# Sorted-block attention feeding a cosine-gated feed-forward: other products, copies and load order for the sorted keys

## The chip, the cores and the metric

The kernel runs on one NeuronCore of one Trainium2 chip. The metric is the device time of one launch in microseconds (us). The core has a matrix engine (TensorE, PE in the profile; its weight loads are a row of their own, PEld), VectorE (DVE), ScalarE (ACT), GpSimd (POOL) and SyncE (SP, which here only issues DMAs). Matrix products are written to PSUM, and VectorE or ACT copy them to the on-chip memory SBUF; GpSimd works on SBUF alone.

## The reference

```python
def _attn_ref(q, k, v, sort_net):                 # (4, 8, 768, 64) each; sort_net (4, 8, 8, 8)
    P = sort_net
    for _ in range(5):                            # balance rows and columns
        P = np.exp(P - np.max(P, axis=-1, keepdims=True))
        P = P / (np.sum(P, axis=-1, keepdims=True) + 1e-09)
        P = P / (np.sum(P, axis=-2, keepdims=True) + 1e-09)
    # k_b, v_b, q_b: 8 blocks of 96 tokens each
    k_sorted = np.einsum('bhij,bhjcd->bhicd', P, k_b)
    v_sorted = np.einsum('bhij,bhjcd->bhicd', P, v_b)
    scores = scale * np.matmul(q_b, k_sorted.transpose(0, 1, 2, 4, 3))
    attn = softmax(scores)                        # within a block
    return np.matmul(attn, v_sorted).reshape(B, H, S, D)

x = attn_out.transpose(0, 2, 1, 3).reshape(3072, 512)
h = x @ w_in                                      # (512, 2048)
out = (h * np.cos(h)) @ w_out                     # (2048, 512)
```

## The kernel before

**Chunks.** The work is cut into eight chunks n = 0 to 7, two for each of the four batches: half of a batch's eight blocks, all eight heads, 384 tokens. For a chunk, `qk` and `qk_half` make the scores of a block u (two head groups, hp = 0 and 1, of four heads h2), `expo` the softmax's exponentials, `av` the weighted values, `moe_up` or `up` the first matrix of the feed-forward with its cosine gate, `moe_down` or `down` the second and the store. The attention of chunk n + 1 is laid by hand between the feed-forward products of chunk n; the order in the file is the order on each engine, which runs its instructions in that order. Waits between engines follow from the tiles. `B` and `C` are the two PSUM pools, `big` with three buffers and `acc` with two; a tile that finds no buffer free waits for the copy that empties the oldest.

**Keys.** The balanced matrix P is laid out as a block-diagonal matrix `bds`; a product with the keys as weights sorts and transposes at once: it takes two tokens (2 x 64 columns) of all blocks and gives, for one block position and head, 64 dims of the first token on PSUM's partitions 0 to 63 and of the second on 64 to 127. The tile `kT[0]` has three zones along its second axis; for scores, head group hp reads zones hp and hp + 1, dims on partitions hp x 64 upward, so that even tokens come from the first of the two and odd ones from the second. For batch 0, `k_sort_0(ih, ...)` works one chunk ih at a time: one product for each two tokens, of 64 rows (batch 0's keys lie on partitions 64 to 127 of `kbuf`), and four copies of 64 partitions for each PSUM tile, two of them from one partition half to the other. It is called four times for chunk 0 (16, 8, 16 and 8 token pairs), at the head of the attention, and three times for chunk 1 (16 pairs each), between the `up` calls of chunk 0. Scores of chunk 0 read only the 64 rows of their own head group. From chunk 1 on the queries lie between zeros, and a score product reads all 128 rows of two zones; what lies in the other half is multiplied by zero, and `z_keys` clears zones 0 and 2 there so that what is multiplied is finite.

For batch 1, `k_sort_1` makes products of 128 rows, in which the matrix holds zeros against batch 0's, and one copy a tile, into zones 0 and 2 with both tokens one above the other; `k_swap` then moves two quarters into zone 1 by two DMAs on SyncE's queue. The same crossing serves batches 2 and 3 (`k_sort_g`, tile `kT2`, which lies over `kT[0]`).

**Loads.** Loads with a change of type go through GpSimd's DMA queue (`load`, `load_pair`, `load_q`, `load_w_in`, `load_w_out`), so they are issued in GpSimd's order, among its copies: `v_permute` regroups the values, `zeros_between` clears what lies between the queries. The keys and values of batches 2 and 3 come as "the second pair". The second pair's values go to `vbuf` in six pieces, right after `v_permute(slice(64, 128))` has read batch 1's values. Chunk 3's query rows come behind them (`load_q(3)`, eight DMAs), and SyncE turns them by two transposing DMAs (`q_transpose_dma(3)`), ahead of the transposing DMAs for chunk 2's softmax (issued in `expo`, line 518) in its queue.

A small trick is used to hold a queue: a GpSimd copy of one column of a tile into `held` makes GpSimd wait until the tile has been written, and all that stands behind it in GpSimd's order with it.

Of the kernel before, what the change touches and what calls it, by code (L numbers as in the profile page):

```python
# [10 lines left out]
FP32 = mybir.dt.float32  # L11
# [7 lines left out]
def kernel(  # L19
# [15 lines left out]
    nc = tc.nc  # L35
    B, H, S, D = q.shape
# [7 lines left out]
    CD = blk * D  # L44
    H2 = H // 2
    NG = B // 2
    NN = 2 * H2 * nb
    IC = 4
# [23 lines left out]
    vbuf, kbuf = kv[:, :CD], kv[:, CD:]  # L72
# [17 lines left out]
    vin_d = v.rearrange("b h (j c) d -> b (h j) (c d)", j=nb)  # L90
# [4 lines left out]
    def load_pair(buf, src, lo, hi):  # L95

        nc.gpsimd.dma_start(
            out=buf[:, lo:hi], in_=src[2:4].rearrange("b r x -> (b r) x")[:, lo:hi])
# [11 lines left out]
    def q_zeroed(n):  # L110

        return kbuf[:blk, :2 * (QZ + D)] if n % 2 else q_mem[:]
# [3 lines left out]
    def where(n):  # L116
        b, ih = n // 2, n % 2
        return b // 2, b % 2, ih

    def load_q(n):  # L120
        b, ih = n // 2, n % 2
        if n < NQ:

            nc.gpsimd.dma_start(
                out=q_rows, in_=q[b][:, ih * IC * blk:(ih + 1) * IC * blk].rearrange(
                    "h (p r) d -> p h (r d)", r=QR))
        else:
            src = q[b].rearrange("h (i c) d -> c i h d", c=blk).rearrange(
                "c i (h e) d -> c i h e d", e=2)
            q_heads = q_zeroed(n).rearrange("p (e x) -> p e x", e=2)[:, :, :QZ].rearrange(  # L130
                "p e (i h w) -> p i h e w", i=IC, h=H2)[:, :, :, :, :D]
            for i in range(IC):
                for e in range(2):
                    nc.gpsimd.dma_start(  # L134
                        out=q_heads[:, i, :, e], in_=src[:, ih * IC + i, :, e])
# [4 lines left out]
    def zeros_between(n):  # L140
        for x in (D, QZ):
            nc.gpsimd.memset(
                q_zeroed(n)[:, x:x + QZ].rearrange("p (x w) -> p x w", w=2 * D)[:, :, :D], 0.0)
# [16 lines left out]
    def load_w_out(z):  # L160
        c = slice(z * FC // 4, (z + 1) * FC // 4)
        nc.gpsimd.dma_start(out=w_out_t[:, c], in_=w_out_d[:, c])
# [23 lines left out]
    kT, kT2 = [kTs[:, :, 0], kTs[:, :, 2]], kTs[:, :, :2]  # L186
# [4 lines left out]
    for i in range(NP):  # L191
        t = const.tile([blk, 2 * H2, 128], BF16, name=f"p_buf{i}")
# [43 lines left out]
    bds = [const.tile([128, 2 * H, nb], BF16, name=f"bd{g}") for g in range(NG)]  # L236
# [49 lines left out]
    def copy_on(eng, dst, src):  # L286
        if eng is nc.scalar:
            eng.copy(dst, src)  # L288
        else:
            eng.tensor_copy(dst, src)  # L290

    V, A = nc.vector, nc.scalar
# [24 lines left out]
    def q_transpose(n, z, engs, pool, tag):  # L317
        for eng, (dst, src) in zip(engs, q_turn(n, z, pool, tag)):
            copy_on(eng, dst, src)
# [8 lines left out]
    held = const.tile([128, 1], FP32, name="held")  # L328
# [28 lines left out]
    MH = H2 * IC  # L357

    def k_products(ps, t, c, rows, rhs, keys=kbuf):
        nc.tensor.matmul(  # L360
            ps[:, t], keys[rows, c * 2 * D:(c + 1) * 2 * D], rhs, start=True, stop=True)

    def k_sort_0(ih, t0, nt, eng, pool, tag):

        ps = pool.tile([128, nt, 2 * MH], FP32, name="ks", tag=tag)
        for t in range(nt):
            k_products(ps, t, t0 + t, slice(64, 128),
                       bds[0][64:, H:, ih * IC:(ih + 1) * IC])
        ms, ts = slice(ih * MH, (ih + 1) * MH), slice(t0, t0 + nt)
        psv = ps.rearrange("p t (e m) -> p e m t", e=2)  # L370
        for hp in range(2):
            for x in range(2):
                copy_on(eng, kT[0][hp * D:(hp + 1) * D, hp + x, ms, ts],
                        psv[x * D:(x + 1) * D, hp])

    k_open = {}

    def k_first(t0, nt, pool, tag):
        ps = pool.tile([128, nt, 2 * MH], FP32, name="ks", tag=tag)
        for t in range(nt):  # L380
            k_products(ps, t, t0 + t, slice(64, 128), bds[0][64:, H:, :IC])
        k_open[t0] = ps.rearrange("p t (e m) -> p e m t", e=2), slice(t0, t0 + nt)

    def k_place(t0, hp, eng):
        psv, ts = k_open[t0]
        for x in range(2):
            copy_on(eng, kT[0][hp * D:(hp + 1) * D, hp + x, :MH, ts],
                    psv[x * D:(x + 1) * D, hp])

    def k_sort_1(t0, eng, pool, tag):  # L390
        ps = pool.tile([128, 8, 2 * NB], FP32, name="ks", tag=tag)
# [14 lines left out]
    def k_swap(keys):  # L406
        nc.sync.dma_start(out=keys[:64, 1], in_=keys[64:, 0])
        nc.sync.dma_start(out=keys[64:, 1], in_=keys[:64, 2])

    def keys_of(n, u, h2, hp):  # L410
        g, b2, ih = where(n)
        z = slice(hp, hp + 2)
        if n < 2:
            return kT[0][:, z, ih * MH + h2 * IC + u]
        m = h2 * nb + ih * IC + u
        return kT[1][:, z, m] if g == 0 else kT2[:, z, b2, m]

# [15 lines left out]
    def v_turn(eng=A):  # L433
        ps = big.tile([128, 128], FP32, name="bdp", tag="big")
        for r in (0, 64):
            nc.tensor.matmul(
                ps[r:r + 64], ident[:, 64 - r:128 - r], bds[0].rearrange("p x i -> p (x i)"),
                start=True, stop=True)
        copy_on(eng, bdv.rearrange("p x i -> p (x i)"), ps[:])
# [4 lines left out]
    def v_sort_b(b, d0, nd, eng, pool, tag):  # L444
        ps = pool.tile([128, nd, 2 * NB], FP32, name="vs", tag=tag)


        rows, xs = slice(0, 64 + b * 64), slice((1 - b) * H, (2 - b) * H)
        for t in range(nd):
            nc.tensor.matmul(  # L450
                ps[:, t], v_cols(d0 + t, b == 1 or d0 + t >= D // 2)[rows],
                bdv[rows, xs].rearrange("p x i -> p (x i)"), start=True, stop=True)
        copy_on(
            eng, vS[0][:, b * 2 * NB:(b + 1) * 2 * NB, d0:d0 + nd],
            ps[:blk].rearrange("p t n -> p n t"))
# [71 lines left out]
    def p_transpose(n, u, eng, pool, tag):  # L527
        p = pb.pop((n, u))
        ps = pool.tile([128, 2 * H2, 128], BF16, name="pps", tag=tag)
        for a in range(2 * H2):  # L530
            nc.tensor.transpose(ps[:blk, a, :blk], p[:, a, :blk], ident[:blk, :blk])  # L531
        copy_on(eng, pT[n, u][:blk], ps[:blk, :, :blk])
# [44 lines left out]
    def up(n, fp, lo=0, hi=TC):  # L577

        h = big.tile([128, 2, 512], FP32, name="h", tag="big")
        w = hi - lo  # L580
        for f2 in range(2):
            f = fp * 2 + f2
            for kk in range(KC):
                nc.tensor.matmul(  # L584
                    h[:, f2, :w], w_in_t[:, kk, f * 128:(f + 1) * 128], xT[n][:, kk, lo:hi],
                    start=(kk == 0), stop=(kk == KC - 1))
        c = cosp.tile([128, 2, TC], FP32, name="c", tag="c")
        nc.scalar.activation(c[:, :, :w], h[:, :, :w], AF.Sin, bias=half_pi[:, 0:1])  # L588
        if lo == 0:
            gt[n, fp] = gp.tile([128, 2, TC], BF16, name="gg", tag="gg")  # L590
        nc.vector.tensor_tensor(  # L591
            gt[n, fp][:, :, lo:hi], c[:, :, :w], h[:, :, :w], op=ALU.mult)
# [51 lines left out]
    B, C = (big, "big"), (acc, "acc")  # L644
# [10 lines left out]
        balance(1)  # L655
        spread(1)

    def z_keys():
        nc.gpsimd.memset(kT[0][64:, 0], 0.0)
        nc.gpsimd.memset(kT[0][:64, 2], 0.0)  # L660

    def z_vperm():
        nc.gpsimd.memset(vperm[:64, :D // 2 * blk], 0.0)

# [16 lines left out]
    load_w_out(1)  # L681
    load_w_out(2)
    load_w_out(3)
    k_sort_0(0, 0, 16, V, *C)
    v_turn()
    k_sort_0(0, 32, 8, V, *B)
    k_sort_0(0, 16, 16, A, *C)
    k_sort_0(0, 40, 8, A, *C)
    v_sort_b(0, 0, 8, A, *C)
    qk(0, 0)  # L690
    qk(0, 1)
# [22 lines left out]
    z_turned(0)  # L714
    last_balance()
    z_vperm()
    z_keys()
    p_transpose(0, 3, V, *C)
    up(0, 0, 0, 2 * blk)
    p_transpose(0, 2, V, *C)  # L720
    up(0, 1, 0, 2 * blk)
    av(0, 2, True)
    up(0, 2, 0, 2 * blk)
    k_sort_0(1, 0, 16, A, *C)
    av(0, 3, True)
    up(0, 3, 0, 2 * blk)
    x_transpose(0, 2, A, *C)
    up(0, 4, 0, 2 * blk)
    up(0, 5, 0, 2 * blk)
    x_transpose(0, 3, A, *C)  # L730
    k_sort_0(1, 16, 16, V, *C)
    up(0, 6, 0, 2 * blk)
    q_transpose(1, 0, (V, V), *C)
    up(0, 7, 0, 2 * blk)
    k_sort_0(1, 32, 16, A, *C)
    up(0, 0, 2 * blk, TC)
    q_transpose(1, 1, (V, V), *C)
    up(0, 1, 2 * blk, TC)
# [11 lines left out]
    load_pair(pair, kin_d, 0 * CD // 2, 1 * CD // 2)  # L750
    load_pair(pair, kin_d, 1 * CD // 2, 2 * CD // 2)
    v_permute(slice(64, 128))
    load_pair(vbuf, vin_d, 0 * CD // 6, 1 * CD // 6)
    load_pair(vbuf, vin_d, 1 * CD // 6, 2 * CD // 6)
    load_pair(vbuf, vin_d, 2 * CD // 6, 3 * CD // 6)
    load_pair(vbuf, vin_d, 3 * CD // 6, 4 * CD // 6)
    load_pair(vbuf, vin_d, 4 * CD // 6, 5 * CD // 6)
    load_pair(vbuf, vin_d, 5 * CD // 6, 6 * CD // 6)
    expo(1, 0, True)
    expo(1, 1, True)  # L760
    down(0, 0, 0, nc.sync)
# [25 lines left out]
    q_transpose(2, 0, (V, V), *B)  # L787
    q_transpose(2, 1, (V, V), *B)
    zeros_between(3)
    load_q(3)  # L790
    up(1, 0)
    v_sort_b(1, 0, 8, A, *C)
# [111 lines left out]
    ts, w = TC // 128 - 1, Dm // 2  # L904
    for z in range(2):
# [6 lines left out]
        for e, (eng, dma) in enumerate((((A, nc.scalar),), ((V, nc.sync), (A, nc.scalar)))[z]):  # L912
            c = slice(e * w // 2, (e + 1) * w // 2) if z else slice(0, w)
# [32 lines left out]
```

## Time and profile before

| what | value |
|---|---|
| three runs | 249.28, 247.25, 249.14 us; median 249.14 |
| the profiled execution | 247.64 us, of which 245.9 span |
| mean granted TensorE clock | 0.949 of full |
| busy over the span | PE 231.3 us (94%), DVE 175.1 (71%), ACT 159.2 (65%), POOL 88.2 (36%) |
| chunk 0's keys, products and copies | 12.79 to 17.04 us |
| chunk 1's keys | 33.4 to 41.8 us |
| batch 1's crossing, issue to the landing of its second DMA | 62.12 to 72.61 us |

The page cuts the span into 40 slices and gives the busy share of each engine; it also lists the chain of work that ended last, followed back from the end, and groups of instructions by line, with what ended the idle time before them. A copy by the helper `copy_on` shows as line 288 (on ACT) or 290 (on VectorE), so it is told apart by its tiles: `kTs<-ks` are the sorted keys. A key product is line 360 (`ks`), a score product line 422 for chunk 0 and 427 otherwise (`sc`). DMAs that GpSimd issues show as POOL instructions with the line of the `dma_start`: 97 for the second pair's, 134 for query rows.

### The profile page before, as it was taken

Reading aid. Unit: us, or ns where it says so; the run is one execution under the profiler, and the core shown is the slowest. Engines: PE = TensorE matmul, PEld = TensorE weight load, DVE = VectorE, ACT = ScalarE, POOL = GpSimd, SP = SyncE. Lnnn points to the kernel's source line nnn. Section 1 sums busy time; section 2 is a strip of 40 time slices with the busy share of each in tenths; the row PEclk is TensorE's granted clock in tenths of the full one; section 3 lists DMA queues with packets and bytes.
Section 4 is the critical chain, followed back from the end, with each engine's and each line's share of the span. In section 5 each row is a group of like instructions: output and inputs, shape, how many; then the busy total and the mean of one; then the engine's idle time right before and its main releaser. Section 6 shows DMA issues by size and latency. Waiting matters only on the chain.

```text
span 245.9 us, 5364 instructions
## 1 busy us (share of the span) xinstructions
PE 231.3 (94%) x2160; PEld 148.5 (60%) x2160; DVE 175.1 (71%) x323; ACT 159.2 (65%) x230; POOL 88.2 (36%) x105
## 2 busy tenths in 40 slices
PE   8879898889979998999999999999999999999994
PEld 6768797656556554665666556655565556445553
DVE  6669668994576866689468996899689768625700
ACT  4469867579277973789578965684578356726611
POOL 6369992499928935310262600800000000000000
PEclk9755589999999999999999999999999999999999
DMA  4999999993998565856697959935490560133012
GB/s 53 235 190 166 182 207 230 200 191 68 174 249 92 71 152 85 100 135 164 179 106 129 67 128 117 231 27 111 103 245 8 112 195 0 32 83 129 0 45 85
DMA packets 67897, 31.20 MB, mean 127 GB/s; under 512 B 56608, under 2 KB 63392, under 8 KB 67616
## 3 DMA queue, kind: packets, MB, share of 16 engines
q0 software_dynamic: 24048, 13.64, 40.5%
q1 hardware_dynamic: 43312, 17.02, 28.9%
q8 instruction: 17, 0.28, 0.5%
q10 hardware_dynamic: 512, 0.20, 0.3%
q14 instruction: 8, 0.07, 0.1%
HBM read 27.27 MB, written 6.29 MB: 137 GB/s over the span
## 4 chain that ended last, share of the span: by engine, by line
PE 73%; DMA 10%; ACT 8%; DVE 6%; issue 2%; SPq 0%; DVEq 0%; ACTq 0%
PE h L584 30%; PE o L608 24%; DMA kTs<-kTs 4%; PE sc L427 4%; PE av L544 3%; PE ks L360 2%; DMA vperm<-p_buf 2%; ACT kTs L288 2%; DMA pT<-p_buf 2%; DVE gg L591 2%; PE pps L531 2%; PE idle L220 2%; ACT p_buf L507 2%; PE vs L460 2%; ACT c L588 1%
## 5 line engine op out<-in xcount | busy, mean ns | idle before, releaser
L584 PE MATMUL h<-xT,w_in_t 128*128 128x384 bf16 (+1 forms) x576 | 92.9, 312 | 0.5 <-DVE gg L591 0.2
L608 PE MATMUL o<-w_out_t,gg 128*128 128x512 bf16 x368 | 88.0, 379 | 0.5 <-DVE s L483 0.5
L588 ACT ACTIVATE c<-h,half_pi 128x768 f32<-128x768 f32 (+1 forms) x72 | 59.6, 830 | 30.0 <-PE h L584 27.6
L591 DVE TENSOR_TENSOR gg<-c,h 128x768 bf16<-128x768 f32 (+1 forms) x72 | 61.2, 860 | 24.2 <-ACT c L588 24.0
L584 PEld LDWEIGHTS <-w_in_t 128*128 128x128 bf16 x576 | 53.8, 100 | 27.4 <-issue 1.4
L608 PEld LDWEIGHTS <-gg 128*128 128x128 bf16 x368 | 33.2, 98 | 32.4 <-DVE s L483 0.7
L483 DVE TENSOR_TENSOR s<-sc,mx 96x384 f32<-96x384 f32 (+1 forms) x43 | 32.2, 749 | 2.7 <-DVE mx L482 0.5
L482 DVE TENSOR_REDUCE mx<-sc 96x4 f32<-96x384 f32 (+1 forms) x43 | 31.9, 743 | 2.7 <-PE sc L427 1.5
L177 POOL COPY vperm<-kv 64x1536 bf16<-64x1536 bf16 (+1 forms) x10 | 28.0, 2843 | 5.5 <-DMA kv<-in_v_dram 5.4
L507 ACT ACTIVATE p_buf<-s 96x768 bf16<-96x768 f32 x32 | 27.7, 896 | 0.6 <-DVE s L483 0.4
L553 DVE TENSOR_TENSOR xn<-av,r 96x512 bf16<-96x512 f32 x32 | 22.0, 687 | 1.1
L288 ACT CAST kTs<-ks 128x512 bf16<-128x512 f32 (+2 forms) x32 | 14.7, 460 | 6.2 <-PE ks L360 6.1
L134 POOL DMA_DIRECT2D kv<-in_q_dram x24 | 16.0, 672 | 6.3 <-DMA kv<-in_v_dram 5.5
L427 PE MATMUL sc<-kTs,q_turned 128*128 128x96 bf16 x224 | 16.1, 206 | 2.2 <-DMA kTs<-kTs 1.3
L551 DVE RECIPROCAL r<-av 96x8 f32<-96x8 f32 x32 | 6.4, 199 | 14.9 <-PE av L544 14.8
L427 PEld LDWEIGHTS <-q_turned 128*128 128x128 bf16 x224 | 12.8, 98 | 6.4 <-issue 1.4
L288 ACT COPY o_s<-o 128x512 f32<-128x512 f32 (+2 forms) x11 | 5.9, 537 | 14.8 <-PE o L608 11.8
L288 ACT COPY kv<-o 128x512 f32<-128x512 f32 x8 | 4.7, 582 | 12.6 <-PE o L608 12.6
L134 POOL DMA_DIRECT2D q_mem<-in_q_dram x16 | 10.6, 673 | 0.3 <-issue 0.3
L588 ACT ACT_TABLE_LOAD x8 | 10.3, 1283 | 0.1
L544 PEld LDWEIGHTS <-pT 96*128 96x128 bf16 (+1 forms) x160 | 7.5, 106 | 4.2 <-DMA pT<-p_buf 1.2
L288 ACT CAST pair<-vs 96x512 bf16<-96x512 f32 (+1 forms) x12 | 8.7, 726 | 2.0 <-PE vs L460 2.0
(101 smaller groups left out, 219.3 us busy)
## 6 DMA issues: line engine op xcount, KB each, us to landing
out_dram<-kv SPq DMA_DIRECT2D x12, 256.0 KB, 3.0
out_dram<-o_s SPq DMA_DIRECT2D x11, 256.0 KB, 2.5
w_in_t<-in_moe_w_in_dram POOLq DMA_DIRECT2D x4, 512.0 KB, 11.4
w_out_t<-in_moe_w_out_dram POOLq DMA_DIRECT2D x4, 512.0 KB, 12.8
kv<-in_k_dram POOLq DMA_DIRECT2D x2, 768.0 KB, 13.3
kv<-in_v_dram POOLq DMA_DIRECT2D x2, 768.0 KB, 15.3
pair<-in_k_dram POOLq DMA_DIRECT2D x2, 768.0 KB, 11.2
kv<-in_v_dram POOLq DMA_DIRECT2D x6, 256.0 KB, 7.3
```

The costliest lines, as they stand in the source:

```text
L134: nc.gpsimd.dma_start(out=q_heads[:, i, :, e], in_=src[:, ih * IC + i, :, e])
L177: nc.gpsimd.tensor_copy(dst, src)
L288: eng.copy(dst, src)
L427: nc.tensor.matmul(out, q_of(n, hp)[:, x:x + 128], keys_of(n, u, h2, hp), start=True, stop=True)
L482: nc.vector.reduce_max(mx[:], scv, axis=AX.X)
L483: nc.vector.tensor_tensor(s_t[n, u][:, part[0]:part[0] + w], scv, mx.to_broadcast([blk, w, H2, blk]), op=ALU.subtract)
L507: nc.scalar.activation(dst, src, AF.Exp, scale=scale)
L553: nc.vector.tensor_tensor(xn.rearrange("p h e d -> p e h d"), avv[:, :, :, :D], r.to_broadcast([blk, 2, H2, D]), op=ALU.mult)
L584: nc.tensor.matmul(h[:, f2, :w], w_in_t[:, kk, f * 128:(f + 1) * 128], xT[n][:, kk, lo:hi], start=(kk == 0), stop=(kk == KC - 1))
L588: nc.scalar.activation(c[:, :, :w], h[:, :, :w], AF.Sin, bias=half_pi[:, 0:1])
L591: nc.vector.tensor_tensor(gt[n, fp][:, :, lo:hi], c[:, :, :w], h[:, :, :w], op=ALU.mult)
L608: nc.tensor.matmul(o[:], gt[n, f // 2][:, f % 2, ts * 128:(ts + 1) * 128], w_out_t[:, f, :], start=(f == 0), stop=(f == FC - 1))
```

## The change

Chunk 0's keys are made by `k_pairs`: for each token one product of 64 rows and 64 columns per head group, the first into PSUM's partitions 0 to 63 and the second into 64 to 127, so that both tokens of both groups already lie where the scores want them, and one copy a tile moves all. Chunk 1's keys are made by `k_cross`: the products stay, one copy a tile goes to zones 0 and 2 as for batch 1, and two GpSimd copies of 64 partitions fill zone 1. `z_keys` goes, since both halves of zones 0 to 2 are now written. The six loads of the second pair's values move behind `zeros_between(3)`, and a new `hold_keys` ahead of them makes GpSimd wait there for batch 1's crossing.

```diff
--- before.py
+++ after.py
@@ -360,32 +360,30 @@
         nc.tensor.matmul(
             ps[:, t], keys[rows, c * 2 * D:(c + 1) * 2 * D], rhs, start=True, stop=True)
 
-    def k_sort_0(ih, t0, nt, eng, pool, tag):
+    def k_pairs(t0, nt, eng, pool, tag):
+
+        ps = pool.tile([128, nt, 2, MH], FP32, name="ks", tag=tag)
+        for t in range(nt):
+            for x in range(2):
+                c = (t0 + t) * 2 + x
+                for hp in range(2):
+                    nc.tensor.matmul(
+                        ps[hp * D:(hp + 1) * D, t, x], kbuf[64:, c * D:(c + 1) * D],
+                        bds[0][64:, H + hp * H2:H + (hp + 1) * H2, :IC],
+                        start=True, stop=True)
+        copy_on(
+            eng, kT[0][:, :2, :MH, t0:t0 + nt],
+            ps.rearrange("p t x m -> p x m t"))
+
+    def k_cross(t0, nt, eng, pool, tag):
 
         ps = pool.tile([128, nt, 2 * MH], FP32, name="ks", tag=tag)
         for t in range(nt):
-            k_products(ps, t, t0 + t, slice(64, 128),
-                       bds[0][64:, H:, ih * IC:(ih + 1) * IC])
-        ms, ts = slice(ih * MH, (ih + 1) * MH), slice(t0, t0 + nt)
-        psv = ps.rearrange("p t (e m) -> p e m t", e=2)
-        for hp in range(2):
-            for x in range(2):
-                copy_on(eng, kT[0][hp * D:(hp + 1) * D, hp + x, ms, ts],
-                        psv[x * D:(x + 1) * D, hp])
-
-    k_open = {}
-
-    def k_first(t0, nt, pool, tag):
-        ps = pool.tile([128, nt, 2 * MH], FP32, name="ks", tag=tag)
-        for t in range(nt):
-            k_products(ps, t, t0 + t, slice(64, 128), bds[0][64:, H:, :IC])
-        k_open[t0] = ps.rearrange("p t (e m) -> p e m t", e=2), slice(t0, t0 + nt)
-
-    def k_place(t0, hp, eng):
-        psv, ts = k_open[t0]
-        for x in range(2):
-            copy_on(eng, kT[0][hp * D:(hp + 1) * D, hp + x, :MH, ts],
-                    psv[x * D:(x + 1) * D, hp])
+            k_products(ps, t, t0 + t, slice(64, 128), bds[0][64:, H:, IC:])
+        ms, ts = slice(MH, 2 * MH), slice(t0, t0 + nt)
+        copy_on(eng, kT[0][:, ::2, ms, ts], ps.rearrange("p t (e m) -> p e m t", e=2))
+        nc.gpsimd.tensor_copy(kT[0][:D, 1, ms, ts], kT[0][D:, 0, ms, ts])
+        nc.gpsimd.tensor_copy(kT[0][D:, 1, ms, ts], kT[0][:D, 2, ms, ts])
 
     def k_sort_1(t0, eng, pool, tag):
         ps = pool.tile([128, 8, 2 * NB], FP32, name="ks", tag=tag)
@@ -407,11 +405,17 @@
         nc.sync.dma_start(out=keys[:64, 1], in_=keys[64:, 0])
         nc.sync.dma_start(out=keys[64:, 1], in_=keys[:64, 2])
 
+    def hold_keys():
+
+        nc.gpsimd.tensor_copy(held[:], kT[1][:, 1, 0, :1])
+
     def keys_of(n, u, h2, hp):
         g, b2, ih = where(n)
         z = slice(hp, hp + 2)
-        if n < 2:
-            return kT[0][:, z, ih * MH + h2 * IC + u]
+        if n == 0:
+            return kT[0][:, :2, h2 * IC + u]
+        if n == 1:
+            return kT[0][:, z, MH + h2 * IC + u]
         m = h2 * nb + ih * IC + u
         return kT[1][:, z, m] if g == 0 else kT2[:, z, b2, m]
 
@@ -655,10 +659,6 @@
         balance(1)
         spread(1)
 
-    def z_keys():
-        nc.gpsimd.memset(kT[0][64:, 0], 0.0)
-        nc.gpsimd.memset(kT[0][:64, 2], 0.0)
-
     def z_vperm():
         nc.gpsimd.memset(vperm[:64, :D // 2 * blk], 0.0)
 
@@ -681,11 +681,11 @@
     load_w_out(1)
     load_w_out(2)
     load_w_out(3)
-    k_sort_0(0, 0, 16, V, *C)
+    k_pairs(0, 16, V, *C)
     v_turn()
-    k_sort_0(0, 32, 8, V, *B)
-    k_sort_0(0, 16, 16, A, *C)
-    k_sort_0(0, 40, 8, A, *C)
+    k_pairs(32, 8, V, *B)
+    k_pairs(16, 16, A, *C)
+    k_pairs(40, 8, A, *C)
     v_sort_b(0, 0, 8, A, *C)
     qk(0, 0)
     qk(0, 1)
@@ -714,25 +714,24 @@
     z_turned(0)
     last_balance()
     z_vperm()
-    z_keys()
     p_transpose(0, 3, V, *C)
     up(0, 0, 0, 2 * blk)
     p_transpose(0, 2, V, *C)
     up(0, 1, 0, 2 * blk)
     av(0, 2, True)
     up(0, 2, 0, 2 * blk)
-    k_sort_0(1, 0, 16, A, *C)
+    k_cross(0, 16, A, *C)
     av(0, 3, True)
     up(0, 3, 0, 2 * blk)
     x_transpose(0, 2, A, *C)
     up(0, 4, 0, 2 * blk)
     up(0, 5, 0, 2 * blk)
     x_transpose(0, 3, A, *C)
-    k_sort_0(1, 16, 16, V, *C)
+    k_cross(16, 16, V, *C)
     up(0, 6, 0, 2 * blk)
     q_transpose(1, 0, (V, V), *C)
     up(0, 7, 0, 2 * blk)
-    k_sort_0(1, 32, 16, A, *C)
+    k_cross(32, 16, A, *C)
     up(0, 0, 2 * blk, TC)
     q_transpose(1, 1, (V, V), *C)
     up(0, 1, 2 * blk, TC)
@@ -750,12 +749,6 @@
     load_pair(pair, kin_d, 0 * CD // 2, 1 * CD // 2)
     load_pair(pair, kin_d, 1 * CD // 2, 2 * CD // 2)
     v_permute(slice(64, 128))
-    load_pair(vbuf, vin_d, 0 * CD // 6, 1 * CD // 6)
-    load_pair(vbuf, vin_d, 1 * CD // 6, 2 * CD // 6)
-    load_pair(vbuf, vin_d, 2 * CD // 6, 3 * CD // 6)
-    load_pair(vbuf, vin_d, 3 * CD // 6, 4 * CD // 6)
-    load_pair(vbuf, vin_d, 4 * CD // 6, 5 * CD // 6)
-    load_pair(vbuf, vin_d, 5 * CD // 6, 6 * CD // 6)
     expo(1, 0, True)
     expo(1, 1, True)
     down(0, 0, 0, nc.sync)
@@ -787,6 +780,13 @@
     q_transpose(2, 0, (V, V), *B)
     q_transpose(2, 1, (V, V), *B)
     zeros_between(3)
+    hold_keys()
+    load_pair(vbuf, vin_d, 0 * CD // 6, 1 * CD // 6)
+    load_pair(vbuf, vin_d, 1 * CD // 6, 2 * CD // 6)
+    load_pair(vbuf, vin_d, 2 * CD // 6, 3 * CD // 6)
+    load_pair(vbuf, vin_d, 3 * CD // 6, 4 * CD // 6)
+    load_pair(vbuf, vin_d, 4 * CD // 6, 5 * CD // 6)
+    load_pair(vbuf, vin_d, 5 * CD // 6, 6 * CD // 6)
     load_q(3)
     up(1, 0)
     v_sort_b(1, 0, 8, A, *C)
```

## The prediction

> **What bounds the kernel now.** I read the page first (slices, chain), then the chain in order of time from 10 to 56 us and from 56 to 100 us, then the stage table, the queues of GpSimd and SyncE, and groups by shape. The profiled execution took 247.64 us, of which 245.9 are span; the median of the three runs shown is 249.14, 1.50 above it. I work on the profiled execution and add 1.50 at the end. From 52 us to the end TensorE is nearly always busy, so what the change does there is worth only the holes it closes or opens. The three places touched are earlier. The first is chunk 0's keys, where the chain is serial (start, length, what):
>
> ```profile
> 12.39 0.36 DVE bd L282
> ...
> 12.79 0.58 PE ks L360 x16
> ...
> 13.63 0.76 PE ks L360 x24
> ...
> 14.42 0.36 ACT kTs L288
> ...
> 16.77 0.27 ACT kTs L288
> ...
> 17.08 0.80 PE sc L422 x9
> ```
>
> The balanced matrix is ready at 12.75, the first scores run at 17.08. Of the 4.33 us between, products take 1.6 and eight ACT copies 2.6. All this, and everything up to 33 us, runs at half TensorE clock (stage, its length, PE and PEld, DVE, ACT, POOL busy, clock, DMA share, GB/s):
>
> ```profile
> 12.50:17.00 4.50, 2.93 (x59) 2.41 (x59) 3.08 (x9) 3.53 (x10) 2.29 (x2) 0.50 1.08 190
> ...
> 33.00:37.00 4.00, 4.00 (x77) 3.73 (x75) 2.93 (x8) 3.45 (x9) 3.91 (x3) 1.00 1.24 208
> 37.00:48.00 11.00, 9.15 (x138) 7.58 (x134) 10.16 (x21) 7.37 (x15) 2.85 (x5) 1.00 1.13 214
> ```
>
> The second place is chunk 1's keys: TensorE sets 33 to 37, VectorE (10.16 busy of 11.0) sets 37 to 48. The third is batch 1's key crossing and the loads beside it:
>
> ```profile
> 62.66 9.95 DMA kTs<-kTs
> ...
> 72.75 0.33 PE sc L427 x4
> ```
>
> ```profile
> 59.19 3.17 POOL L97 DMA_DIRECT2D kv<-in_v_dram  x6 [0.30 <-POOL vperm L177]
> ...
> 67.11 0.67 POOL L134 DMA_DIRECT2D kv<-in_q_dram  x1 [0.24 <-DMA kv<-in_v_dram]
> 69.06 0.67 POOL L134 DMA_DIRECT2D kv<-in_q_dram  x1 [1.29 <-DMA kv<-in_v_dram]
> 72.48 0.67 POOL L134 DMA_DIRECT2D kv<-in_q_dram  x1 [2.75 <-DMA kv<-in_v_dram]
> 74.38 0.67 POOL L134 DMA_DIRECT2D kv<-in_q_dram  x1 [1.23 <-DMA kv<-in_v_dram]
> ```
>
> The crossing takes 9.95 us beside the six value loads, but TensorE waits for it only 1.34 us before 72.75: that is all it can give. The other lines show that the last four loads of chunk 3's query rows are issued only as the third to the sixth value load have landed.
>
> **Step 1, chunk 0's keys.** 48 products of 64x128 weights and 32 columns become 192 of 64x64 weights and 16 columns; 16 copies become 4. The old products start 27 ns apart (16 in 0.58 with a last one of 0.18). The new form is not in the trace; nearest are the query transposes, which also load 64 weight columns, alternating halves of the array, at the same half clock:
>
> ```profile
> 10.12 0.14 PEld L301 LDWEIGHTS <-q_mem 96*64 96x64 bf16 x2
> ...
> 10.12 0.18 PEld L301 LDWEIGHTS <-q_mem 96*64 96x64 bf16 x3
> ```
>
> Two loads, one in each half, start 13 ns apart and take 128 ns each, so the halves load side by side; the third, behind the first in its half, ends 54 ns after it. A half thus takes a product every 54 ns, both together one every 27 ns. Bounds: 13 ns (nothing but the spacing of starts) and 54 ns (the halves in turn). I take 27, since k_pairs alternates the halves strictly: 192 x 27 = 5.2 us against 1.3.
>
> Copies: a 128x512 cast took 0.68 on VectorE (row at 53.84) and 0.58 on ACT; 128x256 I take at 0.42 and 0.37, from the 64x256 rows of as many elements a partition. The queue, by hand: 64 products from 12.79 to 14.7, VectorE copy to 15.4; v_turn's two (0.25); 32 products to 15.8, copy to 16.25; 64 products to 17.6, ACT copy to 18.2; 32 products to 18.45 (their PSUM buffer has been free since 15.4), ACT copy to 18.85. The eight value products behind them wait for the buffer freed at 18.2 and run to 19.0. First scores at 19.0 instead of 17.08: **+1.9 us**. The fewer copies save nothing, since the last tile's products now end later than all copies did. By 13 ns the copies bound it: scores at 16.65, **-0.4**. By 54 ns the products end at 23.6, the copy at 24.0, scores at 24.1, **+7.0**. Behind 17 us the chain runs through scores, softmax and value copies with waits of hundredths, so the shift is passed on whole.
>
> A rule speaks against this step: the Trainium skill, TensorEngine Tiling (Array Packing), section Performance Considerations, under Instruction Overhead, says each matmul costs some 60 cycles however few columns it has, and warns against tiling a dimension that is already small. At the half clock seen here 60 cycles would be about 50 ns, an estimate from that page, and 192 of them 9.6 us. The trace disagrees so far: old products of 32 columns start 27 ns apart at clock 0.50.
>
> If the dense stage comes 1.9 us later while the clock opens at 33.0 as before, some of it runs at full clock that ran at half; if it opens later by as much or more, the TensorE-bound stretch behind 33 loses half of what it shifts, 0.95. I count 0 and keep +-0.9.
>
> **Step 2, chunk 1's keys.** ACT's two tiles lose 4 x 0.37 for 0.58 each, VectorE's one 4 x 0.42 (1.72 with gaps) for 0.68. The first ACT tile (33.98) lies in the stretch where TensorE is busy 4.00 of 4.00: worth 0. VectorE's tile saves 1.04 where VectorE is the bound. Its one idle time of weight from 37 to 48 is 0.57 before 42.43, waiting for the ACT cosine at 41.81, which stood behind the third tile's copies; that tile ends some 0.9 earlier, so 0.57 goes too. **-1.6 us**; bounds -2.2 (the first tile's 0.6 counts as well) and -0.3 (below). POOL gets six 64x256 copies: 64x1536 took 2.83, so 1.84 ns an element, 0.47, and with a one-element copy's 0.19 some 0.66 each. The two memsets of 2.74 at 34.80 go; both lie ahead of the query load that waits idle 4.59 before 42.19, so neither counts. But the last pair now stands between ACT's copy (about 40.2 on the old clock) and chunk 1's scores (43.15, now 41.5): 40.2 + 1.3 = 41.5, just in time. At double length they cost 1.3 of the gain; that is the -0.3.
>
> **Step 3, the moved loads.** Alone, the crossing is short: batch 2's, of twice the bytes, lands 3.8 and 5.0 us after issue, so I let it land at 66.0. TensorE is ready at 71.4: **-1.34** there. POOL's hold_keys waits for it; behind it on POOL stand the six loads, eight query loads, two memsets and the second permutation (11.28, cover until the hold at 95.0). Loads: the first from 66.2, landed 3.9 later as now; the next came 1.9 apart before the crossing's data mixed in, so the sixth lands at 66.2 + 3.9 + 5 x 1.9 = 79.6, not 74.2. The eighth query load follows; its rows land 2.4 later, 82.1. SyncE's two transposes of them start there instead of 76.80 and hold its queue 3.6, to 85.7. Behind them stand chunk 2's softmax transposes, due at 85.51 and now at 84.2: 1.5 late. SyncE runs them with one store nearly without pause up to 91.9, so the fourth issues at 90.2 rather than 90.66, although its softmax came 1.34 earlier, and lands 4.3 later at 94.5. TensorE stands for it until 95.0 now. So of 1.34 only about **-0.45** is left at 95 us, from where TensorE runs on. Bounds: loads 1.4 apart (the fastest pair), sixth at 77, nothing late, -1.34; loads 2.2 apart (the mean of before, crossing included), sixth at 81.1, fourth transpose 1.6 later, +1.15.
>
> Sum: +1.9 - 1.6 - 0.45 = -0.15, **247.5 on the profiled execution, 249.0 on the median**.
>
> **Rivals.** (a) The halves take turns, 54 ns a product: +7.0 - 1.6 - 0.45 = +4.95, 254.1 on the median, slower. It decides as soon as a product costs over some 40 ns. Against it stand the two side-by-side loads; for it, that these are 64 rows of the same row half, a form the trace lacks. This is the case in which the Trainium skill's 60 cycles would come true. (b) Late queries: step 3 at its upper bound, +1.45, 250.6; SyncE's lack of slack speaks for it, a DMA queue without the crossing against. (c) Products at the spacing of starts, copies bound: -0.4 - 1.6 - 0.45 = -2.45, 246.7, faster; the 54 ns between weight loads speaks against. (d) Loads fast, the crossing's gain kept whole: -1.05, 248.1.
>
> **Chances.** Forecast 0.45, (a) 0.18, (b) 0.17, (c) 0.12, (d) 0.08. About 1%, 2.5 us, is what a measurement of this kernel can tell from no change. Faster by more (below 246.6): half of (c) and the tails of the forecast and (d), 0.12. Slower by more (above 251.6): (a), with the tails of the forecast and (b), for the clock and late POOL copies, 0.28. Within: 0.60. The range runs from 246.2 to 253.6: half of (a) and a little of (c) lie outside. The likeliest case alone: 247.8 to 250.5.
>
> **What would show it.** Right: key products 27 ns apart, first scores near 19.0; four copies for chunk 0 of 0.4 to 0.7; VectorE's key tile 0.68 near 38; the crossing landing some 4 us after issue, no TensorE wait at chunk 2's first scores; query transposes starting 5 us later than 76.8, and TensorE waiting longer before the av near 95. Wrong: product spacing far from 27, a stall of scores behind POOL's crossing copies, query transposes issued before 80, or the clock opening at another time than 33 us with the difference following it.

## The result, and the profile after

In 15 runs each on one chip, the changed kernel took a median of 249.88 us and the kernel before 247.71 us. The ratio is 1.0076, with a 95% interval of 1.0054 to 1.0099: **1.9 us slower** (1.3 to 2.5), where the forecast was a gain of 0.15. The profiled execution of the changed kernel took 249.94 us, of which 248.1 are span; before it was 247.64 and 245.9. Executions that ran long are left out of the ratios, above all one of the changed kernel's 15 (338.33 us) and the profiled one of the version with chunk 0's pairs alone (301.96 us, at a lower granted clock from 37 us on, so that only earlier rows of it are used). The ratios here come with the runs and are not the quotients of the two medians, which differ from them by up to 0.003.

The two spans, cut at the same events, show where the time went. Each row is the length of a stage in the profiled executions, from the trace's starts and ends; the last column is what the prediction's steps put there.

| stage | before | after | difference | forecast |
|---|---|---|---|---|
| start to the balanced matrix (`bd`, end) | 12.74 | 13.20 | +0.46 | 0 |
| to the first maximum of scores | 4.86 | 8.60 | **+3.74** | +1.9 |
| to the first `h` product | 11.02 | 11.01 | 0 | 0 |
| to the last gate (`gg`) of chunk 0 | 22.99 | 21.89 | -1.10 | -1.6 |
| to the first gate of chunk 1 | 18.78 | 18.76 | 0 | 0 |
| to the last gate of chunk 1 | 13.93 | 12.54 | -1.39 | -1.34 |
| to the first gate of chunk 2 | 16.07 | 16.95 | +0.88 | +0.89 |
| to the end | 145.47 | 145.18 | -0.29 | 0 |

One row is far off: chunk 0's keys. Three rows of the changed kernel's chain in order of time (start, length, what), from the middle of the key products:

```profile
15.38 2.34 PE ks L370 x53
17.71 1.44 issue
19.15 1.40 PE ks L370 x29
```

The row that matters is `issue`. TensorE stands for 1.44 us and the profile names nobody that it waits for. The timeline of TensorE says where this is (start, length, line, operation, shape, count, and in brackets the idle time before):

```profile
13.25 1.88 PE L370 MATMUL ks<-bd,kv 64*64 64x16 bf16 x64 [0.28 <-DVE bd L282]
15.05 0.32 PE L440 MATMUL bdp<-bd,ident 128*64 128x128 bf16 x2
15.30 2.41 PE L370 MATMUL ks<-bd,kv 64*64 64x16 bf16 x83
19.15 1.40 PE L370 MATMUL ks<-bd,kv 64*64 64x16 bf16 x45 [1.44 <-issue]
```

64 + 83 = 147 key products, then the hole, then 45 (the two `bdp` products between them turn the balanced matrix). The first tile takes 64 products and the second 32, so product 147 is the 51st of the third tile's 64: in the middle of a tile, between two products that read the same matrix and keys that have long been there and write a tile that is already open. No data and no buffer can be late there. Outside the hole the pace is the forecast one: 64 products in 1.88 us with a last one of 0.2, (1.88 - 0.2) / 63 = 27 ns apart.

The four copies are as forecast too (two on VectorE, two on ACT; start, length, line, operation, shape, count, idle time before):

```profile
15.16 0.69 DVE L290 CAST kTs<-ks 128x512 bf16<-128x512 f32 x1 [1.97 <-PE ks L370]
16.37 0.42 DVE L290 CAST kTs<-ks 128x256 bf16<-128x256 f32 x1 [0.52 <-PE ks L370]
```

```profile
19.73 0.58 ACT L288 CAST kTs<-ks 128x512 bf16<-128x512 f32 x1 [4.05 <-PE ks L370]
20.58 0.37 ACT L288 CAST kTs<-ks 128x256 bf16<-128x256 f32 x1 [0.27 <-PE ks L370]
```

Chunk 1's stage, by the same columns as the stage table shown of before, cut 4.2 us later since the first `h` product comes that much later:

```profile
41.20:52.20 11.00, 10.03 (x160) 8.63 (x156) 10.09 (x21) 6.43 (x12) 8.08 (x9) 1.00 0.91 163
```

Before, VectorE was busy 10.16 of 11 us and TensorE 9.15. VectorE still sets the stage with 10.09, but TensorE gets 0.88 more done in it, and ACT's load falls from 7.37 to 6.43. The clock column cannot be compared in this execution, since the record of the clock's first change is missing from it (eight `h` products take 1.37 us at 32.89). The `h` products themselves show when it came: they start 160 ns apart up to 37.6 us and 82 ns apart from 38.6, and the trace has full clock on record from 37.77, against 33.02 before.

The third place, on GpSimd's queue and then on SyncE's:

```profile
68.76 0.18 POOL L410 CAST held<-kTs 128x1 f32<-128x1 bf16 x1 [6.04 <-DMA kTs<-kTs]
69.21 0.54 POOL L97 DMA_DIRECT2D kv<-in_v_dram  x1 [0.27 <-issue]
...
82.46 0.67 POOL L134 DMA_DIRECT2D kv<-in_q_dram  x1 [0.61 <-DMA kv<-in_v_dram]
```

```profile
65.20 0.49 SPq L405 DMA_DIRECT2D kTs<-kTs  x1
...
84.67 3.61 SPq L147 DMA_TRANSPOSE q_turned<-kv  x2
88.38 3.12 SPq L522 DMA_TRANSPOSE pT<-p_buf  x2
```

The hold works: the first value load is issued 0.45 us after the column copy started. The crossing now lands 2.8 us after issue (the median of its two DMAs; 9.2 before), and TensorE does not wait for it. But the last query load goes out at 82.46 (74.38 before), the query transposes start at 84.67 (76.80 before), and they keep SyncE busy until 88.3. Chunk 2's softmax transposes started at 85.51 before; now they stand behind at 88.38. Of these 2.87 us, 1.68 are the shift of everything so far (chunk 1's last gate ends at 86.00, before at 84.32), and 1.19 are the queue's. What this costs TensorE is in the waits of after, 82 to 98 us (sum, times, longest), against 0.9 in one wait before:

```profile
PE av L548 <- DMA pT<-p_buf: 1.6, 2, 0.8
```

### The profile page after: what moved, and what is told of

It is laid out like the page before. It is cut to its first block, busy times and chain, and to the rows that moved or that the text cites. A ratio compares the mean times of both kernels' runs of the same rounds, so it can differ in the third digit from the quotient of the medians.

```text
span 248.1 us, 5639 instructions
## 1 busy us (share of the span) xinstructions
PE 236.2 (95%) x2304; PEld 153.9 (62%) x2304; DVE 172.1 (69%) x314; ACT 156.0 (63%) x218; POOL 87.9 (35%) x110
## 4 chain that ended last, share of the span: by engine, by line
PE 82%; ACT 5%; DMA 5%; DVE 4%; issue 2%; ACTq 0%; DVEq 0%
PE h L588 33%; PE o L612 27%; PE av L548 3%; PE sc L431 3%; DMA pT<-p_buf 2%; PE ks L370 2%; DMA vperm<-p_buf 2%; PE ks L360 2%; PE pps L535 2%; ACT p_buf L511 2%; PE idle L220 2%; PE sk L262 2%; PE vs L454 2%; PE xps L575 2%; PE vs L464 1%
## 5 line engine op out<-in xcount | busy, mean ns | idle before, releaser
L288 ACT CAST kTs<-ks 128x512 bf16<-128x512 f32 (+1 forms) x20 | 11.4, 570 | 9.3 <-PE ks L360 5.0
L431 PE MATMUL sc<-kTs,q_turned 128*128 128x96 bf16 x224 | 15.9, 206 | 0.7 <-DVE s L487 0.7
```

The costliest lines, as they stand in the source:

```text
L431: nc.tensor.matmul(out, q_of(n, hp)[:, x:x + 128], keys_of(n, u, h2, hp), start=True, stop=True)
```

## The experiments

**The theory** for the hole: TensorE ran out of instructions. The 192 short products use up the listing of instructions faster than the next part of it is brought in, and what brings it in is a DMA that stands among the weight loads. The trace shows such DMAs, of 16 KB, as a queue of their own kind, q8. The counts say that it is TensorE's: 18 of them in this execution for 4608 recorded TensorE instructions, 256 each, and 17 for 4320 before. From 14 to 18 us in the changed kernel, the busy tenths of the DMA engines in 40 slices, and two queues with packets, MB and share:

```profile
DMA  9999999999999999999999999999999999999999
...
q0 software_dynamic: 803, 0.80, 121.6%
q8 instruction: 1, 0.02, 1.5%
```

**The rival**: the pair products themselves cost it (something in how 64-column products in two halves of the array follow one another), or chance, and then neither the place nor the other traffic would matter. For the rest of the change the question was which part gives and which takes.

**Each part alone.** The first run has chunk 0's pairs and nothing else.

```diff
-    k_sort_0(0, 0, 16, V, *C)
+    k_pairs(0, 16, V, *C)
     v_turn()
...
```

> Chunk 0's keys by pairs alone; all else as before. Theory (TensorE runs out of instructions in the 192 products and stands 1.4 to 1.6 us, on top of products 27 ns apart): a hole of over 1 us with no wait named, inside a tile's products, and the first scores some 8 us behind the ready matrix instead of 4.3, so 3.0 to 4.0 us slower than before (ratio 1.012 to 1.016). Rival (the hole is an accident of the one profiled execution): no hole, first scores 6.3 us behind the matrix, 1.9 us slower (1.008).

249.78 against 248.05 us; ratio 1.010 (1.0054 to 1.0146). The interval holds both figures, so the time does not decide; the trace does.

```profile
15.27 2.41 PE L370 MATMUL ks<-bd,kv 64*64 64x16 bf16 x83
19.16 1.39 PE L370 MATMUL ks<-bd,kv 64*64 64x16 bf16 x45 [1.48 <-issue]
```

The hole is there without the other two parts, again after product 147. Chunk 0's keys are the part that costs.

The second has chunk 1's keys alone.

```diff
-    z_keys()
...
-    k_sort_0(1, 0, 16, A, *C)
+    k_cross(0, 16, A, *C)
...
```

> Chunk 1's keys crossed by GpSimd alone; all else as before. Theory (VectorE bounds 37 to 48 us and the crossing copies, 0.4 us each, stay hidden): 1.1 to 1.6 us faster (ratio 0.9935 to 0.9955). Rival (what VectorE gains there is waited off behind it, at the batch 1 key crossing or the softmax transposes near 95 us): within 0.4 us of before (0.9985 to 1.0015).

**245.92 against 248.05 us; ratio 0.9916 (0.9877 to 0.9955): 2.1 us faster**, more than expected, though the interval reaches into what was expected, and better than the kernel before and the changed one. The stage up to chunk 0's last gate is 1.43 us shorter. The surprise is the next one: without any load moved, the TensorE wait of 1.34 for batch 1's crossing is gone as well. Its waits from 60 to 80 us are one row:

```profile
PE av L554 <- DVE kTs L290: 0.4, 1, 0.4
```

The crossing is issued at 60.73 and 61.26 here, 1.4 us before where it was (62.12 and 62.66), but chunk 2's first scores are wanted 1.4 us sooner too (they start at 69.97; before, TensorE was ready for them at 71.41). What is different is the time it takes: its DMAs land 7.5 and 8.1 us after issue, the later one at 69.35, where before they took 8.4 and 10.0 and the later one landed at 72.62. The six value loads beside it start almost when they did (59.05, before 59.19), so it now goes out 2.2 us behind the first of them and not 3.5. That it therefore has fewer of their packets ahead of it is argued from these rows; no run separates it.

The third moves the loads alone, behind `hold_keys`.

```diff
+    hold_keys()
+    load_pair(vbuf, vin_d, 0 * CD // 6, 1 * CD // 6)
...
     load_q(3)
```

> The second pair's value loads behind the key crossing, and nothing else. Theory (the crossing lands 3 us after issue and gives 1.34 us, of which the late query rows of chunk 3 take back 0.8 at the softmax transposes): 0.5 us faster (ratio 0.997 to 0.999), query transposes issued near 81.5 us. Rival (the crossing's gain is lost whole): 0 to 0.5 us slower (1.000 to 1.002).

246.93 against 248.05 us; ratio 0.9988 (0.9952 to 1.0025). This is inconclusive: a gain or a loss of a few tenths is inside the interval. The profiled execution (245.63 us) shows the wait for the crossing gone, the query transposes late as expected, and yet nothing taken back at the softmax transposes, where TensorE waits 0.5 us in place of 0.9:

```profile
80.14 3.59 SPq L147 DMA_TRANSPOSE q_turned<-kv  x2
```

```profile
PE av L548 <- DMA pT<-p_buf: 0.5, 1, 0.5
```

The softmax transposes start 1.32 us after chunk 1's last gate, against 1.19 before. Up to that gate the stage is 1.38 us shorter than before, and the next one, to chunk 2's first gate, 0.35 shorter.

The fourth has both, that is all but the pairs.

> The whole change but for chunk 0's keys, which stay as before. Theory (the loss is chunk 0's alone and the other two parts add): 1.6 to 2.1 us faster than before (ratio 0.9915 to 0.9935), 3.5 us faster than the changed kernel. Rival (the parts share one limit near 95 us): no faster than the better of the two alone (0.995 to 0.998).

246.44 against 248.05 us; ratio 0.9957 (0.993 to 0.9984). It misses what was expected and falls where the rival put it: the moved loads do not add to the gain of chunk 1's part. Between the last gate of chunk 1 and the first of chunk 2 it takes 16.91 us, where chunk 1's part alone takes 15.93, and the rows say why:

```profile
80.11 3.61 SPq L147 DMA_TRANSPOSE q_turned<-kv  x2
```

```profile
PE av L558 <- DMA pT<-p_buf: 1.5, 2, 0.8
```

With chunk 1's part alone the query transposes start at 76.27 and the `pT` wait is 0.8. So the late query rows cost 1.0 us here, and there was nothing left for the moved loads to give. With the loads moved alone the transposes came as late, but chunk 1's last gate, and chunk 2's softmax behind it, came 1.0 us later than here.

**The same gain without the late queries.** The hold and the loads stand behind the query loads.

```diff
     zeros_between(3)
     load_q(3)
+    hold_keys()
+    load_pair(vbuf, vin_d, 0 * CD // 6, 1 * CD // 6)
...
```

> Chunk 0's keys as before, chunk 1's crossed by GpSimd, the second pair's values behind the key crossing and also behind chunk 3's query rows. Theory (what the moved loads take back, they take by the late query rows that hold SyncE's queue): the query transposes are issued before 72 us, no more wait at the softmax transposes than before, and the kernel is 2.4 to 3.0 us faster than before (ratio 0.988 to 0.9905). Rival (the loads cost elsewhere, by DMA traffic or by the second permutation): 1.0 to 1.6 us faster, like the version with the loads ahead of the query rows.

245.94 against 247.08 us; ratio 0.9938 (0.9912 to 0.9965). Again a miss: not better than chunk 1's part alone. The mechanism did what was meant:

```profile
68.78 10.19 SPq L147 DMA_TRANSPOSE q_turned<-kv  x2
82.72 2.55 SPq L532 DMA_TRANSPOSE pT<-p_buf  x2
```

```profile
PE av L558 <- DMA pT<-p_buf: 0.9, 1, 0.9
```

The first query transpose starts at 68.78 and the softmax transposes at 82.72, exactly where chunk 1's part alone has them, and from chunk 0 to chunk 3's first gate the two executions agree within 0.15 us. The late queries are cured, and what remains is that there is no wait for the crossing to take away.

**Is the hole a matter of instructions?** In the changed kernel, 74 products stand ahead of the first key product in TensorE's listing, and 147 key products and two of `bdp` follow before the hole: 223 in all, a weight load and a product each, 446 recorded instructions. If the listing decides, then more instructions ahead must move the hole to an earlier key product, by as many. Eight of the 16 warming products at the start give way to 32 shorter ones, 24 more in all.

```diff
-    keep_warm(16)
+    keep_warm(8)
+    small_idle = big.tile([128, 256], FP32, name="idle", tag="big")
+    for _ in range(32):
+        nc.tensor.matmul(
+            small_idle[:, :64], warm[:], warm[:, :1].to_broadcast([128, 64]), start=True, stop=True)
```

> The changed kernel with 24 more products ahead of everything (8 of the 16 warming products of 256 columns become 32 of 64 columns, so the same streaming time). Theory (the hole comes where TensorE has used up the blocks of 256 instructions that had been fetched, whatever it is computing): the hole of some 1.5 us comes 24 products earlier, after about 29 of the third tile's... counted from the first key product after about 93 instead of 117, so some 0.64 us earlier behind the ready matrix (3.9 instead of 4.5 us). Rival (it belongs to a place in the key tiles or to a buffer): same product, 4.5 us behind the matrix.

It was run once, for its trace:

```profile
12.85 1.87 PE L374 MATMUL ks<-bd,kv 64*64 64x16 bf16 x64 [0.38 <-DVE bd L286]
...
14.91 1.77 PE L374 MATMUL ks<-bd,kv 64*64 64x16 bf16 x59
17.19 2.03 PE L374 MATMUL ks<-bd,kv 64*64 64x16 bf16 x69 [0.52 <-issue]
```

The counts in the expectation were wrong in absolute terms, but the shift came: the hole is after product 64 + 59 = 123, exactly 24 earlier than 147. Counted again, 98 products ahead, 123 of the keys and two of `bdp` are 223: the same 446 instructions. No wait for data would move so. The hole is shorter, 0.52 us, since its DMA came 2.1 us earlier: 14.76 to 15.73 us, instead of 16.86 to 17.83. Half of that is the earlier 256th recorded instruction (13.58 against 14.61); the other half is that the DMA followed it by 1.18 us and not by 2.25, for a reason that was not found. In both, TensorE goes on 1.3 to 1.5 us after that DMA's end (19.15 - 17.83, 17.19 - 15.73).

**Is it late because of the loads?** The first three pieces of `w_in`, whose packets fill the DMA engines at 14 to 18 us, are loaded at 20 us instead.

```diff
-            for z in range(3):
-                load_w_in(z)
...
-    load_w_in(3)
+    for z in range(4):
+        load_w_in(z)
```

> The changed kernel with the first three quarters of w_in loaded only at 20 us, with the fourth, so that the DMA engines have little to do from 13 to 18 us. Theory (the block of instructions comes late because its DMA stands behind load packets: it was served 2.2 us after the 256th instruction): the instruction DMA starts within 0.5 us of the 256th instruction, and the hole shrinks by about as much as that, to under 0.5 us or to nothing. Rival (the time from asking to having it is fixed): hole of 1.2 us or more. The time of the whole tells nothing, since the weights come later.

It was run once. The DMA engines from 14 to 18 us, in the same form as above, and TensorE's timeline:

```profile
DMA  0360000000000000000000000000000000005000
...
q8 instruction: 2, 0.03, 3.0%
...
q0 software_dynamic: 6, 0.00, 0.2%
```

```profile
14.93 3.58 PE L368 MATMUL ks<-bd,kv 64*64 64x16 bf16 x128
```

The hole is gone. The instruction DMA starts at 14.25, within hundredths of the 256th recorded instruction of TensorE (14.24); in the changed kernel it starts at 16.86, 2.25 us after the 256th (14.61). The remaining 128 products run in one piece, (3.58 - 0.2) / 127 = 27 ns apart, so the pair products by themselves have no hole in them. The rival falls.

Two more executions qualify this. The 256th instruction is not the exact trigger: in the two executions with quiet DMA engines timed below, the DMA starts when 232 and 205 have been recorded. And the kernel before had the same late DMA: it starts at 16.31, 3.6 us behind the matrix, and with `w_in` moved at 14.22, 1.1 behind it. Nobody waited for it there, because TensorE reaches its 446th recorded instruction only at 23.24, 6 us after that DMA's end.

**What the hole is worth in time.** The same kernel was timed, beside the changed kernel again and beside the kernel before with the same loads moved.

> The changed kernel with all of w_in loaded at 20 us, timed. Theory (the hole costs its 1.5 us whole, and later weights cost nothing because they are wanted only near 29 us): 1.3 to 1.8 us faster than the changed kernel on the same chip, so 0.2 to 0.8 us slower than before (ratio 1.001 to 1.003). Rival (the later weights cost what the hole gives back): as slow as the changed kernel, 1.006 to 1.009.

> The changed kernel itself, beside the other two: ratio to before 1.006 to 1.009, with the hole of some 1.5 us in the third key tile again. If the hole were an accident of the executions profiled so far, it would be missing or elsewhere.

> The kernel before with all of w_in loaded at 20 us, as a control. Theory (TensorE has no hole there to lose, since it uses 256 instructions in 10 us): no gain, 0 to 0.3 us slower (ratio 0.999 to 1.0015). Rival (quieter DMA engines speed up other things in that stage): 0.5 us faster or more (0.998 or less).

| kernel | median, us | ratio to before (247.51) | interval |
|---|---|---|---|
| changed, `w_in` at 20 us | 248.23 | 1.0048 | 1.0027 to 1.0068 |
| changed, again | 249.60 | 1.0109 | 1.0074 to 1.0144 |
| before, `w_in` at 20 us | 246.49 | 0.9973 | 0.9945 to 1.0001 |

The repetition has its hole after product 147 again:

```profile
19.31 1.39 PE L370 MATMUL ks<-bd,kv 64*64 64x16 bf16 x45 [1.64 <-issue]
```

Moving `w_in` takes 1.0109 - 1.0048 = 0.0061, 1.5 us, off the changed kernel, and 0.0027, 0.7 us, off the kernel before, where no hole is. The control's trace shows another source for its gain. There batch 1's values are loaded behind the moved `w_in`, at 33.45 us and not 28.48; GpSimd waits 9.64 us for them (3.56 before), and so issues the second pair's value loads at 65.56 and not 59.19:

```profile
65.56 3.18 POOL L97 DMA_DIRECT2D kv<-in_v_dram  x6 [0.30 <-POOL vperm L177]
```

The crossing, issued at 62.66 and 63.23, stands ahead of them there and lands 2.8 to 2.9 us after issue, and TensorE's wait of 1.34 for it is gone. The changed kernel had no such wait to lose, so there is no reason to take the 0.7 us off its gain. In the traces, the stage from the matrix to the first maximum of scores goes from 8.81 us in the repetition to 6.95 with `w_in` moved, and stays at 4.86 in the control. So the hole is worth 1.9 us in its stage and some 1.5 us in the time; an estimate from the two intervals, taken as independent, is 0.5 to 2.5. The first row lies between the two expectations; the control comes out where its rival put it, but not by the stage that the rival named. Even without the hole the change does not gain: against the kernel before with the same loads moved, 248.23 / 246.49 = 1.007. The traces of these two say why: chunk 0's keys take 2.09 us more, chunk 1's save 1.77, the late queries cost 1.21, and the crossing has nothing to give, because TensorE does not wait for it in that control either, for the reason just given. (In this pair of executions the control also has a late wait of 1.2 us, told of under what is still open, which hides part of the difference.)

## Why the prediction was wrong, step by step

**Step 1, chunk 0's keys, is the step that failed: its hand-made queue was right in every term it had, and lacked one.** The products came 27 ns apart as taken; the bounds of 13 and 54 ns were not needed. Some of that is luck: in the order of the kernel the query transposes go four into one half and four into the other, and the trace does not name the half, so that the two loads 13 ns apart lay in different halves was inferred. The copies took 0.69, 0.42, 0.58 and 0.37 against 0.68, 0.42, 0.58 and 0.37. With the `w_in` loads out of the way the first scores start at 18.98, 6.16 us behind the matrix; the sum said 19.0 - 12.75 = 6.25. (Before, one score product ran at 16.63 already; 17.08 is where the rest follow. To the first maximum of scores the pairs without the hole cost 2.09 us, where the sum had 1.9.) What the queue took for granted is that TensorE always has its next instruction. In the kernel as changed it did not, for 1.6 us from start to start, and the first scores came at 21.0. That is the step that failed: it put the bringing of instructions at nothing, without a reason, and 1.6 us went there. The Trainium skill, on the page Runtime: NRT & Kernel Launch, section Instruction fetch mechanics, tells of blocks of 256 instructions that the sequencer fetches by its own DMA queue, and calls the cost of crossing a block "mostly hidden". The 16 KB DMAs, one for every 254 to 256 recorded instructions, agree with the blocks. That the cost is hidden held in the kernel before and with quiet DMA engines; in the changed kernel, with full ones, the DMA began 2.25 us after the 256th recorded instruction and was not hidden.

The Trainium skill's rule that the prediction weighed against this step, some 60 cycles a matmul (TensorEngine Tiling (Array Packing), section Instruction Overhead), did not come true: at clock 0.50 the products of 64x64 weights ran 27 ns apart, about half of the 50 ns estimated from it. In each half alone they came 53 ns apart. Rivals (a) and (c) fall with their terms.

**Step 2, chunk 1's keys, was right in place and nearly in size**: -1.10 in the changed kernel, -1.43 alone, forecast -1.6, inside its bounds. (The lower bound counts 0.6 for the first ACT tile, where its own rows give 4 x 0.37 - 0.58 = 0.9.) VectorE's stage relaxed as described. GpSimd's crossing copies took 0.40 us each, not 0.66, and no score waited for them:

```profile
45.23 0.40 POOL L386 COPY kTs<-kTs 64x256 bf16<-64x256 bf16 x1
```

The 0.3 us by which the changed kernel gains less than chunk 1's part alone go with the clock, for which the forecast kept 0.9 either way and named another opening than 33 us as a sign. The repetition of the changed kernel gained 1.77 in this stage, not 1.10. Half clock lasted 4.96 us past the first `h` product in the changed kernel, 2.52 in its repetition and 3.22 with chunk 1's part alone, and the stage took 21.89, 21.22 and 21.56. With the pairs the recorded half clock lasts 27.31 us, in the executions that have the record, against 23.89 without them, while the first `h` products shifted by 2.2 to 4.4 us. This is argued from rows; no run separates it.

**Step 3, the moved loads, was right in size for this pair of executions and wrong in its premise.** In the stage table it gives -1.39 and takes back 0.88, against a forecast of -1.34 and +0.89, and so neither rival (b) nor (d) came. That both figures fit is partly luck, for it came by a somewhat different way: the crossing landed 2.8 us after issue (4 forecast), and the sixth value load at 82.2 (79.6 forecast), behind a hold that came 2.6 us later than forecast (68.8, not 66.2). And with the loads moved alone the late queries took nothing back: from the hold to the query transposes it was 14.9 us there, against 15.9 here and in the forecast, and why was not found. The premise was that only the moved loads could remove the wait for the crossing. That the loads beside it are what makes the crossing long was right: it took 2.7 to 2.9 us with them behind it in the changed kernel, with the loads moved alone, with both parts and in the control, and 7.5 to 10.0 with them beside it. But with chunk 1's part alone the wait is gone too, though the loads stay where they were. Two edits that remove the same wait do not add up, so inside the change the moved loads bring only the late queries, 0.9 to 1.0 us as forecast.

**The sum.** The forecast was +1.9 - 1.6 - 0.45. The trace shows +3.74 for step 1, -1.10, -0.51, +0.46 in the start and -0.29 in the tail. The start need not be the change's doing: 13.20 against 12.74 us to the same matrix, but executions with the pairs have it anywhere from 12.80 to 13.44, and one without them (the kernel before with `w_in` moved) has it at 13.12. In sum this is 2.3 us, of which the hole is 1.6. That 249.88 us lies close to the forecast 249.0 says nothing for it: the forecast stood on the median of three runs, 249.14, and that of fifteen is 247.71. Its range, too, was kept wide for other reasons, halves in turn, late queries and the clock.

**Still open.** Three executions (both versions with chunk 1's part and moved loads, and the kernel before with `w_in` moved) have a wait of 1.2 us near chunk 5, `PE av` for a `vperm<-p_buf` DMA, that the others do not have; it accounts for 1.1 of the 1.7 us between the executions of chunk 1's part alone and of the version with the query loads first, and what calls it up was not found. Whether the moved loads cost anything in time beside chunk 1's part alone is not settled either: 0.9957 and 0.9938 against 0.9916, with intervals that overlap.

## What to carry to other kernels

Split products cost more than their pace: count the instructions too, and where some hundred short ones follow one another while the DMA engines are full, look for a row of "issue" in the middle of a tile, which here was an engine that had run out of instructions. Before crediting an edit with a wait, look whether the wait is still there with the other edits of the same change alone; the same microsecond is given only once. A control can gain for a reason of its own: read its trace before taking its gain off. The part worth keeping here is chunk 1's keys with one copy a tile and GpSimd's crossing, alone: 0.9916 (0.9877 to 0.9955).

## What the runs showed of the hardware

A TensorE that waits for nothing in the profile can be waiting for its instructions. In the versions with the pairs it stood 0.5 to 1.6 us in four executions, each time after 446 recorded instructions, and went on 1.3 to 1.5 us after the end of a 16 KB instruction DMA of about 1 us. With quiet DMA engines that DMA began when 205 to 256 instructions had been recorded, and there was no hole. In those four executions, with the engines full, it began when 328 to 406 had been recorded, 1.2 to 2.4 us after the 256th.

Products with 64 weight columns, alternating between the two column halves, kept 53 ns a half and 27 ns together at half clock; the old products with 128 columns also came 27 ns apart, so four times the products took four times the time (48 in 1.3 us, 192 in 5.2 us by that spacing). The Trainium skill, TensorEngine Tiling (Array Packing), section Restrictions under Tile-to-Partition Mapping, says that column tiling switches off the fast weight load; the 53 ns for 64 columns against 27 ns for 128 agree with that, though no run here separates the cause.
